# Weight conversion from the seventh head on, and two unread products per head instead of one

## The chip, the core and the metric

The program runs on one NeuronCore of a Trainium2 chip; the other seven are not used. The metric is device time in microseconds (us) of one execution, as the median of several runs. In the profile the engines are PE (TensorE, matrix products), DVE (VectorE), ACT (ScalarE), POOL (GpSimd) and SP (SyncE, which here only issues transfers). Each engine works off its own instructions in order; they wait for one another by semaphores.

## What is computed

Three layers: windowed causal attention with a linear bias, a dense layer with squared ReLU, and a layer with eight experts of which each token takes one.

```python
# attention: B, H, S, D = 4, 8, 576, 64; window of 128 positions
scores = scale * np.matmul(q, k.transpose(0, 1, 3, 2))
scores = np.where(mask, scores + bias[None], -1000000000.0)
scores = scores - np.max(scores, axis=-1, keepdims=True)
attn = np.exp(scores)
attn = attn / (np.sum(attn, axis=-1, keepdims=True) + 1e-09)
attn_out = np.matmul(attn, v)
...
# x: 2304 tokens x 512; w_in 512 x 2048, w_out 2048 x 512
h = x @ w_in
r = np.maximum(h, 0.0)
x = (s * (r * r) + b) @ w_out
...
# experts: each token goes to the expert of its largest logit, 512 -> 1024 -> 512
h = np.maximum(x[mask] @ w1[e], 0.0)
out[mask] = gate_w[mask, None] * (h @ w2[e])
```

## The kernel before

The 2304 tokens are 18 tiles of 128. Attention goes by units, one head of one tile: 144 units, eight per tile. One call of `tick` starts a unit and carries earlier ones on by a step each; the tick of unit n does:

- the score product of unit n (`stage_A`, L242, into one of the banks 0 to 3; two products where a unit looks at two key tiles),
- the value product of unit n-4 (`stage_D`, L301), the transposition of unit n-2 (`stage_C`, L278), and for every fourth unit a transposition of finished rows (`stage_T`, L330),
- on DVE the bias and minimum of the scores (`stage_B`, L254), on ACT the exponential with its sum (`stage_N`, L262) and the copy of the transposed weights (`stage_C2`, L283).

The dense weights come as 32 chunks of 512 KB (w_in and w_out by turns) and are held as a high and a low part. `conv_ops` gives four steps for a chunk: the load, issued by SP (L178), into one of four `stage` buffers; a cast on ACT (`cast`, L181); a shift on DVE (`d`, L185); the high part on ACT (L193) with the low part on DVE (L194), both in `e`. The queue `conv` holds these steps in order. `pt`, called seven times per tick in the first four tiles, adds `rate` to a counter and takes the next step from the queue whenever the counter passes one. The loads of the first four chunks are issued at the start, among those of the first tiles of q, k and v.

`warm(n)` issues n products of zeros, 128x512, into bank 3 (L747); nobody reads them, which is why they are called unread products here. Nine stand ahead of the first tick.

The first four ticks (`LEAD`) stand under `manual_schedule`, which keeps their instructions in the order of the text. Everything else of this stage may be moved by the scheduler: it puts an instruction on its engine where its own model of the time finds it ready, also ahead of instructions that the text has earlier. The ticks up to `ticks(2)`, 21 of them, go with nothing beside them; from then on the first dense products (`L1`, L351: twelve products for a block of w_in; `L2`, L374: six for a block of w_out) are mixed with two ticks per block. `need(c)` takes conversion steps until chunk c is done, before a product that reads it.

Of the kernel before, what the change touches and what calls it, by code (L numbers as in the profile page):

```python
# [43 lines left out]
def moe_attention_kernel(ctx, tc, qT, kT, vN, w_in, w_out, sc_s, sc_b, bneg, tri, bmix,  # L44
# [190 lines left out]
    def stage_A(u, S):  # L235
        t, h, order, sl, bc, n = geom(u)
        pr, odd = divmod(h, 2)
        hb = slice(64, 128) if odd else slice(0, 64)
        o = S[:, 0:n]
        if t < NRAW:  # L240
            for i, k in enumerate(order):
                nc.tensor.matmul(S[:, i * P:(i + 1) * P], lhsT=raws[1][t][hb, pr, :], rhs=raws[0][k][hb, pr, :], start=True, stop=True)  # L242
            return
        Q, K, L = (sp.QO, sp.KO, sp.LO) if odd else (sp.QE, sp.KE, sp.LE)
        nc.tensor.matmul(o, lhsT=Q[:, pr, :], rhs=K[:, pr, sl, :], start=True, stop=False)
        nc.tensor.matmul(o, lhsT=Q[:, pr, :], rhs=L[:, pr, sl, :], start=False, stop=True)

    def stage_B(u, S):
        t, h, order, sl, bc, n = geom(u)
        s, st = sbuf(u)[:, 0:n], st_r[u % 4]  # L250
        bi, c = (bias8[h], -0.125) if t < NRAW else (bias, 2.0 ** -(h + 1))
        if t in MIXED or t in AFTER_MIXED:
            bi, bc = bmx[t in AFTER_MIXED], slice(0, 256)
        nc.vector.tensor_tensor_reduce(s, S[:, 0:n], bi[:, bc], scale=c, scalar=3.0e38,  # L254
                                       op0=ALU.add, op1=ALU.min, accum_out=st[:, 0:1])
# [18 lines left out]
    def stage_C(u, PO):  # L274
        t, h, order, sl, bc, n = geom(u)
        p = sbuf(u) if t < NRAW else sp.p[u % 2]
        for i in range(len(order) if t < NRAW else 1):
            nc.tensor.transpose(PO[:, i * 128:(i + 1) * 128], p[:, i * 128:(i + 1) * 128], ident)  # L278
# [15 lines left out]
    def stage_D(u, PO):  # L294
        t, h, order, sl, bc, n = geom(u)
        last = len(order) - 1
        if t < NRAW:
            o = outs(u)[:, h % 4 * 64:(h % 4 + 1) * 64]
            for i, k in enumerate(order):
                v = raws[2][k].rearrange("p c f -> p (c f)")[:, h * 64:(h + 1) * 64]  # L300
                nc.tensor.matmul(o, lhsT=PW[u % 2][:, i * P:(i + 1) * P], rhs=v, start=i == 0, stop=i == last)  # L301
            return
        for i, k in enumerate(order):
            nc.tensor.matmul(PO[:, 0:P], lhsT=sp.V[k % 3][:, h // 2, :], rhs=PP[u % 2][:, t - k], start=i == 0, stop=i == last)

    def stage_X(u, PO, part=2):
        t, h = divmod(u, H)
        if t < NRAW:
            if h % 4 == 3 and part != 0:
                g = u // 4 % 2  # L310
                rs, xs = rs_r[g], xs_r[g]
                nc.vector.tensor_scalar(rs, su_r[t % 2][:, h - 3:h + 1], 1e-9, None, op0=ALU.add)
                nc.vector.reciprocal(rs, rs)
                nc.vector.tensor_tensor(xs.rearrange("p (h d) -> p h d", h=4), outs(u).rearrange("p (h d) -> p h d", h=4),
                                        rs.unsqueeze(2).to_broadcast([P, 4, 64]), op=ALU.mult)
            return
        pr, odd = divmod(h, 2)
        hb = slice(64, 128) if odd else slice(0, 64)
        blk, c = divmod(t, 2)
        xh, xl = (x[hb, pr, c * P:(c + 1) * P] for x in xbuf(blk))  # L320
        o = PO[hb, 0:P]
        if part != 1:
            nc.scalar.activation(xh, o, AF.Copy)
        if part != 0:
            nc.vector.tensor_tensor(xl, o, f32(xh), op=ALU.subtract)

    def stage_T(u):
        g = u // 4 % 2
        for i in range(2):
            nc.tensor.transpose(bank[4 + g][:, 256 + i * P:256 + (i + 1) * P], xs_r[g][:, i * P:(i + 1) * P], ident)  # L330

    def stage_Y(u):
        t, g = u // H, u // 4 % 2
        blk, c = divmod(t, 2)
        o = bank[4 + g][:, 256:512].rearrange("p (c t) -> p c t", c=2)
        xh, xl = (x[:, 2 * g:2 * g + 2, c * P:(c + 1) * P] for x in xbuf(blk))
        nc.scalar.activation(xh, o, AF.Copy)
        nc.vector.tensor_tensor(xl, o, f32(xh), op=ALU.subtract)
# [69 lines left out]
    def run(ops):  # L408
        for f in ops:
            if callable(f):  # L410
                f()
# [173 lines left out]
    rate, due = [0.0], [0.0]  # L585
# [9 lines left out]
    def plan_preps(t, h):  # L595

        if t < NRAW:
            return
        if h in (0, 1):
            preps.ops += prep_q(t, 2 + h)  # L600
            if h == 1 and t + 1 < NT:
                preps.ops.append(lambda: load_qkv(t + 1, 1))
        if t + 1 < NT:
            if h == HK:
                preps.ops += prep_k(t + 1)
                if t + 2 < NT:
                    preps.ops.append(lambda: load_qkv(t + 2, 0))
            if h == HV:
                preps.ops.append(lambda: load_qkv(t + 1, 2))
            if h in (5, 6):  # L610
                preps.ops += prep_q(t + 1, h - 5)
# [11 lines left out]
    def unit(n):  # L623

        n -= LAG if n >= NRAW * H + LAG else 0
        return n if 0 <= n < UN else None

    def ticks(t):

        return t * H + LAG + (LAG - 1 if t > NRAW else 0)  # L630

    OR0, OR, OR1 = 'BX.C.M.G.N...', '.BUC..VME.G[..R]', 'BUC.VE...MG[].R.'
    def tick(Sb, POb, mid=None, attend=True, Ob=None):
        n = nu[0] if attend else 2 * UN
        if attend:
            nu[0] += 1
        u, c, d, x = (None if NRAW * H <= i < NRAW * H + LAG else unit(i) for i in (n, n - 2, n - LAG + 1, n - LAG))
        if u is not None:
            S = Sb[u % len(Sb)]
            plan_preps(*divmod(u, H))  # L640
            stage_A(u, S)
        if d is not None:
            POd = Ob[d % len(Ob)] if Ob else POb[d % len(POb)][:, 256:512]
            stage_D(d, POd)
        if c is not None:
            POc = POb[c % len(POb)]
            stage_C(c, POc)
        turn = x is not None and x % 4 == 3 and x < NRAW * H
        if turn:
            stage_T(x)  # L650
        def B():
            if u is not None:
                stage_B(u, S)

        def X():
            if d is not None:
                stage_X(d, POd)

        def U():
            if d is not None:  # L660
                stage_X(d, POd, 0)

        def V():
            if d is not None:
                stage_X(d, POd, 1)

        def C():
            if c is not None:
                stage_C2(c, POc)

        def N():
            if u is not None:
                stage_N(u)
            if turn:
                stage_Y(x)

        def E():
            if u is not None:
                stage_N(u, 0)
            if turn:  # L680
                stage_Y(x)

        def R():
            if u is not None:
                stage_N(u, 1)

        def M():
            if mid is not None:
                mid(0)

        def G():
            if mid is not None:
                mid(fill if '[' in od else ())
            elif '[' in od:
                run(fill)

        fs = dict(E=E, R=R, U=U, V=V, B=B, X=X, C=C, N=N, M=M, G=G)
        od = OR0 if n < NRAW * H else (OR if mid is not None else OR1)
        fill = [pt if z == '.' else fs[z] for z in od[od.find('[') + 1:od.find(']')]] if '[' in od else []
        od = od[:od.find('[') + 1] + od[od.find(']') + 1:]  # L700
        for z in od:
            if z == '[':
                continue
            if z == '.':
                pt()
            else:
                fs[z]()
# [18 lines left out]
    HK, HV = 2, 5  # L726
    SK = 8
    J3 = 4
    LEAD = 4

    def need(c):
# [12 lines left out]
    def warm(n):  # L744

        for _ in range(n):
            nc.tensor.matmul(bank[3], lhsT=zero[:, 0:P], rhs=zero, start=True, stop=True)  # L747

    warm(9)
    with tc.manual_schedule():  # L750
        for i in range(LEAD):
            tick(*wide)
            warm(1)
            if i == 1:
                rate[0] = 0.17
    for i in range(LEAD, ticks(2)):
        tick(*wide)
        warm(1)
    rate[0] = 0.4
    for j in range(SK):  # L760
        def mid(i):
# [14 lines left out]
    for j in range(SK):  # L776
        first(1, j)
        if j >= J3:
            tick(**third_b)
# [6 lines left out]
        pt()  # L786
        if j == J3 - 1:
            while preps.ops:
# [312 lines left out]
```

## Time and profile before

| | |
|---|---|
| time of 3 runs, median (lowest to highest) | 914.15 us (914.04 to 915.16) |
| time of the profiled execution | 915.15 us |
| span in the profile, first to last instruction | 913.4 us |
| mean granted clock of PE over the span | 0.959 |
| PE busy | 896.0 us, 98% |
| ACT, DVE, POOL busy | 647.0, 642.2, 325.4 us |

The profile gives for a stretch of time the busy time of each engine and the granted clock of PE, as a share of full speed. Two levels occur: 1.00 is 2.4 GHz, 0.50 is 1.2 GHz; a number between them is a stretch with both. A row of the timeline is an instruction, or several alike run together (x4), with its start and its time; where the engine was idle ahead of it, the row ends with that idle time and what released the instruction. The time of a product in the timeline includes its way through the array, so consecutive products overlap; what a product costs in a row of products is the distance of two starts.

### The profile page before, as it was taken

The page shows a single profiled execution, that of the slowest core. Times are in us where ns is not written, and L with a number is a line of the kernel's source. Part 1 is how long each engine was busy: PE and PEld are TensorE (multiplying, and loading weights), DVE is VectorE, ACT ScalarE, POOL GpSimd, SP SyncE. Part 2 cuts the span into 40 slices and gives each one's busy share as a digit, 9 for nine tenths or more (in the row PEclk, how much of TensorE's full clock was granted, in tenths as well). Part 3 has the DMA queues.
Part 4 walks back from the last instruction along what each step waited for, and adds up shares of the span by engine and source line. Part 5 has one row for each costly group of instructions (what it writes and reads, how often), then busy time and mean ns, then how long its engine had stood idle before and what let it go on. Part 6 is the DMA issues. An engine that isn't in the chain of part 4 may idle for free. (4 is left out here: it accounts for less than half of the span.)

```text
span 913.4 us, 17128 instructions
## 1 busy us (share of the span) xinstructions
PE 896.0 (98%) x5341; PEld 777.2 (85%) x5344; DVE 642.2 (70%) x1719; ACT 647.0 (71%) x1501; POOL 325.4 (36%) x553
## 2 busy tenths in 40 slices
PE   7999998999999999999999999999999999999997
PEld 4678877989999999999999999988888888888886
DVE  3336789656665676667666655467989999899895
ACT  4447897656676767666776753457889889888885
POOL 2000246554663266555655642111632111111101
PEclk7558999999999999999999999999999999999999
DMA  7224652010020102011200200456973795755300
GB/s 263 74 70 134 227 161 78 13 59 13 25 59 13 59 24 59 21 31 44 58 16 33 36 1 1 168 184 227 268 262 127 267 338 212 257 187 210 110 20 29
DMA packets 31600, 101.32 MB, mean 111 GB/s; under 512 B 8581, under 2 KB 9222, under 8 KB 24850
## 3 DMA queue, kind: packets, MB, share of 16 engines
q1 hardware_dynamic: 26562, 89.58, 29.4%
q0 software_dynamic: 4256, 9.46, 2.9%
q10 hardware_dynamic: 688, 1.15, 0.3%
q8 instruction: 43, 0.70, 0.3%
q14 instruction: 51, 0.42, 0.2%
HBM read 133.82 MB, written 10.92 MB: 158 GB/s over the span
## 5 line engine op out<-in xcount | busy, mean ns | idle before, releaser
L351 PE MATMUL bank<-XH,WIH 128*128 128x256 f32 x576 | 173.3, 301 | 0.8 <-ACT r L361 0.8
L351 PE MATMUL bank<-XH,WIL 128*128 128x256 f32 x576 | 163.7, 284 | 0.0
L351 PE MATMUL bank<-XL,WIH 128*128 128x256 f32 x576 | 163.4, 284 | 0.0
L363 DVE SCALAR_TENSOR_TENSOR bank<-bank,s_sb,r 128x256 f32<-128x256 f32 x112 | 55.1, 492 | 108.6 <-ACT r L361 108.2
L374 PE MATMUL bank<-WOH,GH 128*128 128x512 f32 x288 | 118.9, 413 | 0.5 <-ACT GH L364 0.5
L374 PE MATMUL bank<-WOH,GL 128*128 128x512 f32 x288 | 115.5, 402 | 1.1 <-DVE GL L366 1.1
L374 PE MATMUL bank<-WOL,GH 128*128 128x512 f32 x288 | 114.7, 398 | 0.0
L351 PEld LDWEIGHTS bank<-XH,WIH 128*128 128x128 f32 x576 | 110.6, 192 | 3.0 <-ACT r L361 1.0
L351 PEld LDWEIGHTS bank<-XL,WIH 128*128 128x128 f32 x576 | 110.4, 192 | 1.9 <-issue 0.2
L351 PEld LDWEIGHTS bank<-XH,WIL 128*128 128x128 f32 x576 | 109.9, 191 | 0.0
L364 ACT ACTIVATE GH<-bank,b_sb 128x256 fp32r<-128x256 f32 x112 | 53.2, 475 | 69.5 <-DVE bank L363 69.5
L262 ACT ACTIVATE s<-s,st 128x256 f32<-128x256 f32 (+1 forms) x144 | 71.2, 494 | 20.9 <-DVE st L254 17.7
L361 ACT ACTIVATE r<-bank 128x256 f32<-128x256 f32 x144 | 54.0, 375 | 44.5 <-PE bank L351 42.5
L830 PE MATMUL bank<-WIH,XH 128*128 128x512 f32 x192 | 77.7, 405 | 0.0
L254 DVE CUSTOM_DVE_ANT_0 s<-bank,bias 128x256 f32<-128x256 f32 (+1 forms) x112 | 44.7, 400 | 46.3 <-PE bank L242 32.5
L832 PE MATMUL bank<-WIL,XH 128*128 128x512 f32 x192 | 75.8, 395 | 0.0
L831 PE MATMUL bank<-WIH,XL 128*128 128x512 f32 x192 | 75.7, 394 | 0.0
L975 POOL DMA_INDIRECT out<-x,ids x23 | 28.1, 1223 | 133.4 <-ACT XH L959 109.3
L272 POOL TENSOR_SCALAR p<-p,st 128x128 f32<-128x128 f32 x104 | 42.5, 408 | 85.7 <-DVE st L265 69.7
L830 PE MATMUL bank<-WOH,XH 128*128 128x512 f32 x176 | 71.2, 405 | 0.0
L832 PE MATMUL bank<-WOL,XH 128*128 128x512 f32 x176 | 69.5, 395 | 0.0
L831 PE MATMUL bank<-WOH,XL 128*128 128x512 f32 x176 | 69.4, 394 | 0.0
(190 smaller groups left out, 2361.6 us busy)
## 6 DMA issues: line engine op xcount, KB each, us to landing
W1R<-w SPq DMA_DIRECT2D x46, 1024.0 KB
W2R<-w SPq DMA_DIRECT2D x46, 1024.0 KB
stage<-w_in SPq DMA_DIRECT2D x16, 512.0 KB
stage<-w_out SPq DMA_DIRECT2D x16, 512.0 KB
raw<-kT SPq DMA_DIRECT2D x18, 256.0 KB
raw<-qT SPq DMA_DIRECT2D x18, 256.0 KB
x1d<-stage SPq DMA_DIRECT2D x7, 512.0 KB
V<-vN SPq DMA_DIRECT2D x10, 256.0 KB
```

The source lines that it names most:

```text
L254: nc.vector.tensor_tensor_reduce(s, S[:, 0:n], bi[:, bc], scale=c, scalar=3.0e38, op0=ALU.add, op1=ALU.min, accum_out=st[:, 0:1])
L262: nc.scalar.activation(s, s, AF.Exp, bias=st[:, 0:1], scale=-1.0, accum_out=su)
L272: nc.gpsimd.tensor_scalar(p, p if n > P else s, st[:, 3:4], 1.0, op0=ALU.mult, op1=ALU.mult)
L351: nc.tensor.matmul(o, lhsT=w[j][:, c * P:(c + 1) * P], rhs=x[:, c, :], start=n == 0, stop=n == 11)
L361: nc.scalar.activation(r, o, AF.Relu)
L363: nc.vector.scalar_tensor_tensor(q, x, s_sb, r, op0=ALU.mult, op1=ALU.mult)
L364: nc.scalar.activation(gh, q, AF.Identity, bias=b_sb)
L374: nc.tensor.matmul(acc[k], lhsT=a[:, ts], rhs=w[j], start=(j == 0 and i == 0), stop=(j == NF - 1 and i == 2))
L830: nc.tensor.matmul(o, lhsT=lh, rhs=hi, start=first, stop=False)
L831: nc.tensor.matmul(o, lhsT=ll, rhs=hi, start=False, stop=False)
L832: nc.tensor.matmul(o, lhsT=lh, rhs=lo, start=False, stop=last)
L975: nc.gpsimd.indirect_dma_start(out=out[:, :], out_offset=bass.IndirectOffsetOnAxis(ids[:, 0:1], 0), in_=y, in_offset=None, bounds_check=NT ...
```

## The change

Conversion no longer begins in the third tick but in the seventh (`CONV = 6`, counted from zero), at a rate of 0.25 steps per call of `pt` instead of 0.17; the rate in the ticks behind this stage is as it was. Each of the first 21 ticks is followed by two unread products instead of one. In the new text all conversion of this stage is asked for outside the four ticks of `manual_schedule`. Line numbers behind L729 grow by one: the unread products are L747 before and L748 after.

```diff
@@ -726,6 +726,7 @@
     HK, HV = 2, 5
     SK = 8
     J3 = 4
+    CONV = 6
     LEAD = 4
 
     def need(c):
@@ -750,12 +751,12 @@
     with tc.manual_schedule():
         for i in range(LEAD):
             tick(*wide)
-            warm(1)
-            if i == 1:
-                rate[0] = 0.17
+            warm(2)
     for i in range(LEAD, ticks(2)):
+        if i == CONV:
+            rate[0] = 0.25
         tick(*wide)
-        warm(1)
+        warm(2)
     rate[0] = 0.4
```

What the scheduler makes of it shows in the order of the instructions on each engine. ACT at the start of the program, before; `stage_95` and `stage_96` are the buffers of the first chunk of w_in and the first of w_out, `s_...` the scores of a unit, `PW_...` copies of transposed weights:

```order
L535 ACTIVATE su_184<-half 128x2
L262 ACTIVATE s_165,su_184<-s_165,st_167 128x128
L262 ACTIVATE s_166,su_184<-s_166,st_168 128x128
L181 ACTIVATE tmp_156<-stage_96 128x512
L283 ACTIVATE PW_190<-bank_82 128x128
L262 ACTIVATE s_192,su_184<-s_192,st_169 128x128
L181 ACTIVATE tmp_155<-stage_95 128x512
```

The same place of ACT after:

```order
L535 ACTIVATE su_184<-half 128x2
L181 ACTIVATE tmp_155<-stage_95 128x512
L193 ACTIVATE WIH_113<-stage_95 128x512
L262 ACTIVATE s_165,su_184<-s_165,st_167 128x128
L262 ACTIVATE s_166,su_184<-s_166,st_168 128x128
L283 ACTIVATE PW_190<-bank_82 128x128
L262 ACTIVATE s_192,su_184<-s_192,st_169 128x128
L181 ACTIVATE tmp_156<-stage_96 128x512
```

Before, two exponentials come first and then the cast of the second chunk; after, the cast and the high part of the first chunk come ahead of the first exponential, and the cast of the second chunk follows the third one.

DVE at the start of the program after (before, the two upper conversion rows stand further down, behind the fifth and the sixth score reduction):

```order
L530 MEMSET zero 128x256
L185 SCALAR_TENSOR_TENSOR stage_95<-stage_95,tmp_155 128x512
L194 TENSOR_TENSOR WIL_121<-stage_95,WIH_113 128x512
L254 ISA s_165,st_167<-bank_78,bias_176 128x128
L254 ISA st_167 128x1
```

The shift and the low part of the first chunk now stand ahead of the first score reduction.

PE around its second value product (`PW_191`), before; `bank_81` takes the unread products, `zero` is their operand:

```order
L242 MATMUL bank_79<-raw_0_194,raw_0_197 128x128
L301 MATMUL bank_85<-raw_0_200,PW_191 128x64
L278 MATMUL bank_85<-ident,s_165 128x128
L747 LDWEIGHTS zero
L747 MATMUL bank_81<-zero 128x512
L242 MATMUL bank_80<-raw_0_194,raw_0_197 128x128
L278 MATMUL bank_82<-ident,s_166 128x128
L301 MATMUL bank_85<-raw_0_200,PW_190 128x64
L747 LDWEIGHTS zero
L747 MATMUL bank_81<-zero 128x512
```

PE at the same value product after, from the last two of four unread products in a row:

```order
L748 LDWEIGHTS zero
L748 MATMUL bank_81<-zero 128x512
L748 LDWEIGHTS zero
L748 MATMUL bank_81<-zero 128x512
L301 MATMUL bank_85<-raw_0_200,PW_191 128x64
L278 MATMUL bank_85<-ident,s_165 128x128
L748 LDWEIGHTS zero
L748 MATMUL bank_81<-zero 128x512
L748 LDWEIGHTS zero
L748 MATMUL bank_81<-zero 128x512
L278 MATMUL bank_82<-ident,s_166 128x128
L301 MATMUL bank_85<-raw_0_200,PW_190 128x64
```

The two score products between these steps have moved ahead of them, and the unread products have come closer together: four, two and (behind the last row) two more, with two short steps between each.

## Rows read from the trace of the kernel before

**Rows 1.** The page: PE's busy total, and granted clock in 40 slices (tenths).

```profile
PE 896.0 (98%) x5341; PEld 777.2 (85%) x5344; DVE 642.2 (70%) x1719; ACT 647.0 (71%) x1501; POOL 325.4 (36%) x553
...
PEclk7558999999999999999999999999999999999999
```

**Rows 2.** Stretches: length, busy us (count) of PE PEld DVE ACT POOL; clock, DMA.

```profile
8.70:12.30 3.60, 0.02 (x1) 0.00 (x0) 0.09 (x1) 0.90 (x3) 0.00 (x0) 1.00 1.04 417
...
14.00:30.00 16.00, 15.64 (x50) 9.99 (x50) 5.88 (x24) 7.54 (x26) 0.00 (x0) 0.50 0.48 163
30.00:62.80 32.80, 32.09 (x118) 24.15 (x121) 11.16 (x38) 14.31 (x41) 0.00 (x0) 0.50 0.22 67
62.80:72.30 9.50, 9.50 (x39) 8.16 (x40) 4.58 (x11) 5.48 (x13) 0.00 (x0) 0.50 0.25 72
...
77.40:100.00 22.60, 22.53 (x152) 18.88 (x152) 18.39 (x48) 19.39 (x48) 0.00 (x0) 1.00 0.57 180
```

**Rows 3.** Timeline of PE: start, us, instruction, and idle time before it.

```profile
8.39 0.33 PE L278 MATMUL bank<-ident,s 128*128 128x128 f32 x1
12.35 0.56 PE L301 MATMUL bank<-raw,PW 128*128 128x64 f32 x2 [3.63 <-ACT PW L283]
...
16.80 0.47 PE L278 MATMUL bank<-ident,s 128*128 128x128 f32 x1
```

**Rows 4.** Timeline of ACT: two steps of conversion.

```profile
11.40 0.77 ACT L181 ACTIVATE tmp<-stage 128x512 f16<-128x512 bf16 x1 [3.81 <-DMA stage<-w_out]
...
14.28 0.66 ACT L193 ACTIVATE WIH<-stage 128x512 fp32r<-128x512 f32 x1
```

**Rows 5.** Stretches around a later idle time of PE.

```profile
150.00:151.90 1.90, 0.00 (x0) 0.02 (x1) 1.87 (x5) 1.85 (x6) 1.82 (x4) 1.00 0.03 9
...
152.50:155.80 3.30, 3.30 (x11) 2.72 (x10) 2.10 (x6) 2.53 (x7) 3.07 (x7) 0.50 0.14 47
155.90:158.00 2.10, 2.10 (x19) 2.06 (x19) 1.97 (x10) 0.48 (x2) 0.96 (x3) 1.00 0.45 163
```

**Rows 6.** Timeline of PE: first and last of six dense products; another first.

```profile
73.81 0.63 PE L374 MATMUL bank<-WOH,GH 128*128 128x512 f32 x1
...
75.94 0.63 PE L374 MATMUL bank<-WOH,GL 128*128 128x512 f32 x1
...
152.46 0.78 PE L374 MATMUL bank<-WOH,GH 128*128 128x512 f32 x1
```

**Rows 7.** Timeline of SP: an issue.

```profile
8.02 0.33 SPq L546 DMA_DIRECT2D b_sb<-sc_b  x1
```

**Rows 8.** SP's waits up to 30 us: what that issue waited for.

```profile
SPq L546 <- DMA stage<-w_in: 1.2, 1, 1.2
```

**Rows 9.** Timeline of DVE: first score reduction; two steps of conversion.

```profile
6.03 0.29 DVE L254 CUSTOM_DVE_ANT_0 s<-bank,bias 128x128 f32<-128x128 f32 x1 [4.90 <-POOL bias L553]
...
12.21 0.69 DVE L185 SCALAR_TENSOR_TENSOR stage<-stage,tmp 128x512 uint32<-128x512 uint32 x1 [4.41 <-ACT tmp L181]
...
15.26 0.69 DVE L194 TENSOR_TENSOR WIL<-stage,WIH 128x512 fp32r<-128x512 f32 x1
```

**Rows 10.** Timeline of PE: one head at half clock, score product to unread product.

```profile
47.54 1.22 PE L242 MATMUL bank<-raw,raw 64*128 64x128 f32 x4
...
50.02 0.63 PE L747 MATMUL bank<-zero 128*128 128x512 bf16 x1
```

**Rows 11.** Timeline of PE: the steps of a head at full clock.

```profile
82.86 0.71 PE L242 MATMUL bank<-raw,raw 64*128 64x128 f32 x4
...
84.13 0.37 PE L351 MATMUL bank<-XH,WIH 128*128 128x256 f32 x1
```

**Rows 12.** Timeline of PE: first product of three blocks of w_in.

```profile
62.81 0.56 PE L351 MATMUL bank<-XH,WIH 128*128 128x256 f32 x1
...
72.38 0.56 PE L351 MATMUL bank<-XH,WIH 128*128 128x256 f32 x1
...
90.11 0.37 PE L351 MATMUL bank<-XH,WIH 128*128 128x256 f32 x1
```

## The prediction

> **What bounds the kernel now.** First the page: PE is busy for 98% of the span, so what PE has to do sets the time, unless its clock is low. The line of the granted clock has its only long low stretch at the start [rows 1]. The stretches show it: from 14.00 to 62.80 and on to 72.30 the clock is 0.50, its lower level (1.2 GHz), while PE is busy nearly throughout and ACT less than half of the time; from 77.40 it is 1.00 (2.4 GHz) [rows 2]. So for some 65 us the kernel is bound by PE at half clock. That is the stage the change touches: the first 21 heads (16 of the first two tiles and 5 behind them) and the first dense products after them.
>
> How the clock was lost is in the timeline. PE stops behind a transposition of 8.39 and starts again at 12.35, after 3.63 us of waiting for ACT [rows 3]. In 8.70 to 12.30 it is idle, still at 1.00, and afterwards the clock is 0.50 [rows 2]. ACT in that time stood before the cast of a conversion (L181), waiting until 11.40 for a weight load [rows 4]; the copy L283 that PE's row names was queued behind it. A shorter hole far later confirms the pattern: PE idle in 150.00 to 151.90, then 152.50 to 155.80 at 0.50, then 1.00 again [rows 5]. What ran before a return: six 512-column products back to back, 73.81 to 75.94, start to start 2.13/5 = 0.426 us [rows 6]; the clock is 1.00 from about 77.4. The same products begin at 152.46 [rows 6] and lead to the return by 155.90 [rows 5]. Heads with one unread product each, and later heads mixed with L351, ran from 14.00 to 72.30 without a return [rows 2].
>
> One rule of the Trainium skill would tell this otherwise. "TensorE: Matmul & The Clock Gate", Part 1, says that "the default state is throttled, and activity releases the throttle". Here a busy PE (15.64 of 16.00 us and 32.09 of 32.80 [rows 2]) was not released. By the rule alone half clock would end soon after each restart, which is the second rival below; by the rows it matters what PE is busy with.
>
> **The change, part by part.**
>
> (1) The start of conversion. The text puts it at the seventh head, but the order of the changed kernel has the first conversion whole (cast, shift, high part, low part) at the head of ACT and DVE, ahead of the first softmax. So the blocked ACT does not go away. The first weight load has landed when SP's waiting issue starts at 8.02; the wait's releaser is that load [rows 7, 8]. Then, in series, cast 0.77 and high part 0.66 on ACT [rows 4], shift 0.69 and low part 0.69 on DVE [rows 9]: 8.1 to 8.9, 9.6, 10.3, 11.0. Only then comes the first score reduction (L254, 6.03 now [rows 9]), 0.29 long, and PE's fourth score product needs its bank. PE restarts at about 11.4 instead of 12.35. It stopped not later than now (8.39 + 0.33), about 7.6 by its shorter list (three score products, four unread ones): a hole of 2.7 us at least, 3.8 by count. The hole at 150.00 was 1.90, so the clock falls again. I count no gain from the moved start but the restart, 0.95 us.
>
> (2) Lateness. Ahead of the hole the old order also ran two score products and two transpositions that now come after it. Six such products of a wide head take 50.02 - 47.54 = 2.48 us at half clock, 0.41 each [rows 10], so 1.65 us. Between restart and the transposition of the fifth head there are eight unread products instead of three: 5 x 0.426 = 2.13. That transposition, at 16.80 now [rows 3], comes at 16.80 - 0.95 + 1.65 + 2.13 = 19.6.
>
> (3) What the doubled products do to the clock. Between restart and 19.6 the new order has four unread products in a row, a value product, a transposition, two unread, a transposition, a value product, two unread: eight of 0.426, 3.4 us, in about 4.6 us. Nothing between 14.00 and 73.81 is like it in the trace (one unread product stands there after 2.48 us of head steps [rows 10], and the L351 are broken up by head steps). It is nearer to the dense products that stood ahead of the two returns than to the 58 us that brought none. I take the return to 1.00 to fall in or right behind this cluster, at 19.6; bounds: at the restart (11.4) and not before the dense products (72 to 87). This is the main choice of the forecast; the trace does not show this mix.
>
> (4) The rest of the stage at full clock. From 16.80 to the first L351 at 62.81 [rows 3, 12] PE needs 46.0 us now, 15 unread products within it (6.4 us), 39.6 without. The head steps shrink from 2.48 to 84.13 - 82.86 = 1.27 [rows 10, 11], factor 0.51: 20.3 us. The 30 unread products that remain cost half of 0.426 each, 6.4: 26.7 us. The second product per head, so, costs 3.2 us here. ACT, off the path now, is nearly late next: busy 7.54 + 14.31 us in 14.00 to 62.80 [rows 2], plus the greater rate of conversion (15 heads x 7 x 0.25 = 26.3 steps instead of 19 x 7 x 0.17 = 22.6; 3.7 steps at about 0.7, from 0.77 and 0.66 [rows 4]): about 24 us. In 77.40 to 100.00 ACT was busy 19.39 of 22.60 and PE still never idle [rows 2]; at that share 24 us need 28. I take 28 (26.7 if ACT hides, 30 if PE waits a little for each copy). First L351 at 19.6 + 28 = 47.6 instead of 62.81: 15.2 us gained.
>
> (5) The first dense stage. From L351's start of one weight block to the next at half clock: 72.38 - 62.81 = 9.57; at full clock 90.11 - 84.13 = 5.98 [rows 11, 12]. The 14.6 us from 62.81 to 77.4 shrink by the factor 0.625: 5.5 us gained. No cost for weights: their loads go ahead as before on SP's queue and DMA is not full there.
>
> (6) Conversion is about one weight block further when the heads end; this relieves ACT later by at most 0.77 + 0.66 = 1.4 us, in a stage that PE bounds at 22.53 of 22.60. I take 0 and keep 1.4 for the lower end.
>
> Sum: 915.15 (profiled execution, span 913.4 and 1.75 around it) - 15.2 - 5.5 = 894.5. The profiled execution lies 1.0 above the median shown, within the spread of the runs. I round to 895.
>
> **Rivals.**
>
> A, slower: no return in the heads. Then all the unread products after the hole, 38 instead of 18, run at half clock on a PE that is the bound: 20 x 0.426 = 8.5; plus 1.65, less 0.95: the first L351 at 72.0, 9.2 us late. The clock comes back with dense products. In the new order the twelve L351 of the first block are unbroken, so it may come 4 to 12 us earlier in the sequence than now, worth 0.375 of that, 1.5 to 4.5. Time 919.5 to 924, middle 922. It decides whether the clock is 1.00 or 0.50 between 20 and 60 us. For it: 58 us of busy PE without a return. Against it: no dense cluster stood in them.
>
> B, faster still: full clock soon after the restart, as the skill's sentence quoted above has it, or no fall in the hole. The 8.2 us from 11.4 to 19.6 then shrink by about 0.4: 891. Against it: rows 2 and 5.
>
> C: the clock returns in the cluster, PE runs ahead of ACT, waits for a copy or for a load that ACT waits for (as in rows 4), and falls to half again for a part of the heads. Half of the gain of (4) lost: 902 to 910. Against it: from 77.40 to 100.00 the kernel kept 1.00 with ACT at 86% [rows 2].
>
> D, the change does what it says: no conversion ahead of the first softmax, no hole at all. The order excludes it.
>
> **How the numbers follow.** Forecast with return in the cluster 0.58 (889 to 902: return some 4 us earlier or later at 0.4, ACT's bounds, the 1.4 of (6)); A 0.24; B 0.08; C 0.08; D 0.02. The cases of both signs hold much, so the range reaches from B's lower end, 888, to the middle of A, 922; what is left out is the upper half of A and a little below. Faster by over 0.2% (about what a measurement of this kernel can tell from no change): all but A and a little of C, 0.73. Within 0.2%: 0.03. Slower: 0.24.
>
> **What would show it.** In the profile after: ACT's first L181 at about 8.1 and the first L254 at about 11.0; PE idle until 11.4; clock 0.50 behind that; 1.00 again by 16 to 23; the first L351 near 48; the stages behind 100 us unchanged but some 20 us earlier. If the clock stays at 0.50 until L351, step 3 is wrong and A holds, and each unread product shows 0.43 start to start. If PE never idles early, step 1 is wrong. If 1.00 holds but the first L351 is later than 52, ACT's share in step 4 is wrong.

## The result and the profile after

| | before | after |
|---|---|---|
| median (lowest to highest) | 914.10 us (913.08 to 915.16) | 890.95 us (890.56 to 891.63) |
| profiled execution | 915.15 us | 890.56 us |
| span; mean granted clock | 913.4 us; 0.959 | 888.8 us; 0.992 |

The ratio is 0.9747 [0.9731, 0.9764]: 23 us faster, 4 us below the forecast of 895 and inside its range. In all the times below a ratio leaves out the executions that lie over 1.5% above the fastest of their kernel; the medians and ranges count them.

PE's busy total has become smaller although the change adds 21 products, and the low slices of the clock at the start are nearly gone. The page after (compare [rows 1]):

```profile
PE 874.3 (98%) x5365; PEld 759.5 (85%) x5365; DVE 641.5 (72%) x1719; ACT 647.3 (73%) x1501; POOL 321.4 (36%) x553
...
PEclk8999999999999999999999999999999999999999
```

Stretches after, with the columns of [rows 2]:

```profile
8.00:10.00 2.00, 0.00 (x0) 0.00 (x0) 1.28 (x2) 0.66 (x1) 0.22 (x1) 1.00 1.04 421
...
11.00:12.00 1.00, 1.00 (x5) 0.26 (x3) 0.00 (x0) 0.90 (x5) 0.00 (x0) 0.71 1.03 352
12.00:14.00 2.00, 2.00 (x8) 1.49 (x8) 0.66 (x5) 1.47 (x7) 0.00 (x0) 0.50 0.16 35
...
18.00:20.00 2.00, 2.00 (x12) 1.29 (x12) 1.27 (x4) 1.47 (x6) 0.00 (x0) 0.94 1.04 374
...
30.00:40.00 10.00, 10.00 (x66) 6.92 (x64) 7.48 (x21) 8.62 (x23) 0.00 (x0) 1.00 0.30 84
...
127.50:130.80 3.30, 3.30 (x12) 2.73 (x11) 3.17 (x9) 2.84 (x8) 3.06 (x5) 0.50 0.01 2
```

The hole is there (no PE work in 8.00 to 10.00). The clock falls behind it: 0.71 in 11.00 to 12.00 is full clock until 11.00 + (0.71 - 0.50)/0.50 = 11.42, then 0.50. It is back soon: 0.94 in 18.00 to 20.00 is half clock for 2 x (1 - 0.94)/0.50 = 0.24 us, so the return lies at 18.24. From there on it is 1.00 up to 127.5, where a stretch at 0.50 follows an idle time of PE, as at 152.5 before [rows 5]; another of the same length stands at 574.7 to 578.0 (before at 599.6 to 603.0). Half clock behind the hole lasted 6.8 us instead of the 65 us of [rows 2].

PE after (restart, the cluster, one head at full clock, and the first dense product), then ACT, SP and DVE during the hole:

```profile
10.44 0.70 PE L242 MATMUL bank<-raw,raw 64*128 64x128 f32 x4 [3.14 <-DVE st L254]
...
14.46 1.89 PE L748 MATMUL bank<-zero 128*128 128x512 bf16 x4
...
16.67 1.06 PE L748 MATMUL bank<-zero 128*128 128x512 bf16 x2
17.52 0.42 PE L278 MATMUL bank<-ident,s 128*128 128x128 f32 x1
...
18.06 0.70 PE L748 MATMUL bank<-zero 128*128 128x512 bf16 x2
...
28.57 0.71 PE L242 MATMUL bank<-raw,raw 64*128 64x128 f32 x4
...
29.93 0.59 PE L748 MATMUL bank<-zero 128*128 128x512 bf16 x2
30.45 0.71 PE L242 MATMUL bank<-raw,raw 64*128 64x128 f32 x4
...
45.51 0.36 PE L351 MATMUL bank<-XH,WIH 128*128 128x256 f32 x1
```

```profile
6.95 0.78 ACT L181 ACTIVATE tmp<-stage 128x512 f16<-128x512 bf16 x1 [4.27 <-DMA stage<-w_in]
8.79 0.66 ACT L193 ACTIVATE WIH<-stage 128x512 fp32r<-128x512 f32 x1 [1.06 <-DVE stage L185]
```

```profile
6.88 0.33 SPq L546 DMA_DIRECT2D b_sb<-sc_b  x1
```

```profile
SPq L546 <- DMA stage<-w_in: 0.7, 1, 0.7
```

```profile
7.77 0.99 DVE L185 SCALAR_TENSOR_TENSOR stage<-stage,tmp 128x512 uint32<-128x512 uint32 x1 [6.63 <-ACT tmp L181]
9.48 0.69 DVE L194 TENSOR_TENSOR WIL<-stage,WIH 128x512 fp32r<-128x512 f32 x1 [0.72 <-ACT WIH L193]
10.09 0.28 DVE L254 CUSTOM_DVE_ANT_0 s<-bank,bias 128x128 f32<-128x128 f32 x1
```

In the cluster the pair of 16.67 takes 1.06 us, a half-clock distance of 0.43; the pair of 18.06, the last of the cluster, takes 0.70. The conversion of the first chunk stands ahead of the first score reduction, in series between ACT and DVE from 6.95 to 10.1, and PE waits for it.

### The profile page after: what moved, and what is told of

It is laid out like the page before. It is cut to its first block, busy times and chain, and to the rows that moved or that the text cites. A ratio compares the mean times of both kernels' runs of the same rounds, so it can differ in the third digit from the quotient of the medians.

```text
span 888.8 us, 17171 instructions
## 1 busy us (share of the span) xinstructions
PE 874.3 (98%) x5365; PEld 759.5 (85%) x5365; DVE 641.5 (72%) x1719; ACT 647.3 (73%) x1501; POOL 321.4 (36%) x553
## 5 line engine op out<-in xcount | busy, mean ns | idle before, releaser
L351 PE MATMUL bank<-XH,WIH 128*128 128x256 f32 x576 | 172.3, 299 | 1.0 <-ACT r L361 0.8
L351 PE MATMUL bank<-XH,WIL 128*128 128x256 f32 x576 | 163.0, 283 | 0.0
L351 PE MATMUL bank<-XL,WIH 128*128 128x256 f32 x576 | 162.2, 282 | 0.0
L351 PEld LDWEIGHTS bank<-XH,WIH 128*128 128x128 f32 x576 | 109.3, 190 | 4.0 <-ACT r L361 2.2
L351 PEld LDWEIGHTS bank<-XL,WIH 128*128 128x128 f32 x576 | 109.6, 190 | 1.5
L351 PEld LDWEIGHTS bank<-XH,WIL 128*128 128x128 f32 x576 | 108.9, 189 | 0.2
L374 PEld LDWEIGHTS bank<-WOH,GL 128*128 128x128 f32 x288 | 54.5, 189 | 15.2 <-DVE GL L366 3.4
```

The source lines that it names most:

```text
L351: nc.tensor.matmul(o, lhsT=w[j][:, c * P:(c + 1) * P], rhs=x[:, c, :], start=n == 0, stop=n == 11)
L374: nc.tensor.matmul(acc[k], lhsT=a[:, ts], rhs=w[j], start=(j == 0 and i == 0), stop=(j == NF - 1 and i == 2))
```

## The experiments

All of them compute the same outputs; lines are those of the changed kernel, or of the kernel before where a version is made from that. The question was fourfold: which of the two parts of the change brings the gain, what about the unread products brings the clock back, whether they are needed afterwards, and what the hole costs. The kernel before, run again beside them, had medians from 912.2 to 914.1 us; a difference of 1 or 2 us between versions that ran at different times says little.

**The conversion part alone.**

```diff
-            warm(2)
+            warm(1)
...
-        warm(2)
+        warm(1)
```

> The changed kernel with one unread product per head instead of two: the conversion part of the change alone. Theory (clock lost in the early hole, brought back by the dense cluster of unread products): ACT and DVE start with the first conversion as in the changed kernel, PE idles until about 10.4 us, the clock is 0.50 from there to the first dense blocks, first L351 at 60 to 63 us, time 911 to 915 us. Rival (the moved conversion makes the gain, by a freer ACT): clock back within the heads, 890 to 896 us.

Measured 906.64 us (904.55 to 913.57, seven runs), ratio 0.994 [0.9906, 0.9974]. The profiled execution (910.38) has the hole (PE waits 3.9 us for L254), and stretches like those of before:

```profile
20.00:40.00 20.00, 20.00 (x73) 14.29 (x72) 7.57 (x26) 8.16 (x27) 0.00 (x0) 0.50 0.27 85
...
70.00:80.00 10.00, 10.00 (x59) 8.38 (x59) 8.14 (x19) 7.15 (x17) 0.00 (x0) 0.88 0.48 166
```

Half clock stays until about 72. The moved conversion alone is worth 0.6%, and it doesn't remove the hole. The stretches are those that were expected; the median is 4.4 us below the expected 911 to 915.

**The doubled products alone** (the kernel before with both of its `warm(1)` made `warm(2)`).

```diff
-            warm(1)
+            warm(2)
...
-        warm(1)
+        warm(2)
```

> The kernel before with two unread products per head: the other part alone, conversion from the third head at 0.17. In its order three exponentials and a copy come ahead of the first cast on ACT, so the wait for the first chunk (landed by 7 to 8 us) blocks little. Theory: the hole shrinks to under 1.5 us or goes, the clock stays at 1.00 or returns in the cluster of four, two and three unread products; 885 to 892 us. Rival (the moved conversion makes the gain): half clock to the dense blocks and 20 unread products more on it, 919 to 924 us.

Measured 883.64 us (883.23 to 883.88), ratio 0.9681 [0.9647, 0.9714]: better than the whole change by 7.3 us. There is no hole. The only wait of PE up to 60 us is the one at the opening:

```profile
PE bank L747 <- DVE zero L530: 1.2, 1, 1.2
```

The timeline of ACT in this kernel shows where the first cast stands:

```profile
8.64 0.28 ACT L283 ACTIVATE PW<-bank 128x128 f32<-128x128 f32 x1 [0.50 <-PE bank L278]
...
9.20 0.77 ACT L181 ACTIVATE tmp<-stage 128x512 f16<-128x512 bf16 x1
```

The cast stands behind the first copy and the third exponential, and finds its load landed: it has no idle time ahead of it. Before, a cast stood ahead of that copy and waited until 11.40 [rows 4]; that was the cast of the second chunk, whose load is issued later, while here the first cast is that of the first chunk, as the expectation above read it from the order (the row doesn't name the chunk). With more work on PE the scheduler gave the cast a later place. So in the whole change the two parts work against each other: the conversion part puts a blocking step first, and the doubled products are paid for bringing the clock back. Of the 7.3 us between the two kernels 5.1 are there at the first dense product (L351 at 40.40 here, 45.51 in the whole change, with the same head steps ahead of it). The waiting of 3.14 and half of the 6.8 us at half clock, 3.4, would make 6.5; the opening, where the distance of the products falls to 0.21 at about 6.5 us here and at 4.6 in the whole change, takes about 1 off the difference. The other 2.2 come later; the stretches at 0.50 of 127.5 and 574.7 are missing in this profile, which reads 1.00 from 60 to 880.

**Two products in the first nine heads, then one** (of the changed kernel).

```diff
-        warm(2)
+        warm(2 if i < 9 else 1)
```

> The changed kernel, two unread products behind the first nine heads, one behind the other twelve. Theory (once back, the clock is kept by what the heads do with one product): 1.00 from about 18 us on, twelve products of 0.21 less on PE, 888 to 891 us. Rival (two per head are needed to keep it): falls to 0.50 again between 20 and 45 us, 896 to 908 us.

Measured 887.62 us (884.98 to 889.18), ratio 0.9714 [0.9676, 0.9751]; 3.3 us less than the whole change. The hole is there (3.4), the return at about 19.7, and behind it the clock is kept with one product per head:

```profile
16.00:20.00 4.00, 4.00 (x14) 2.18 (x12) 1.48 (x6) 1.52 (x6) 0.00 (x0) 0.54 0.95 335
20.00:40.00 20.00, 20.00 (x131) 14.70 (x130) 12.94 (x44) 16.17 (x50) 0.00 (x0) 1.00 0.37 113
```

**Two in the first nine heads, then none.**

```diff
-        warm(2)
+        warm(2 if i < 9 else 0)
```

> The changed kernel with two unread products in the first nine heads and none in the twelve behind them (these products are read by nothing). Theory: the clock returns in the cluster of eight unread products as in the version with two and then one (by about 20 us), and PE that runs its heads back to back does not need unread products to keep it; then a further 12 x 0.213 = 2.6 us fall away where PE bounds, so 885 us, or 887 to 888 where ACT's copies come next to bound the heads. Rival: without unread products PE runs ahead of ACT and DVE, stands still for a copy, and the clock falls again: 0.50 for a part of the heads and 895 to 910 us.

Measured 885.25 us (883.13 to 895.98, four runs), ratio 0.9728 [0.9665, 0.9791]. With a longer hole in the profiled execution (4.5 us) the return comes at 21.1; then PE is never idle for long and the clock stays without any unread product:

```profile
20.00:22.00 2.00, 2.00 (x8) 1.07 (x7) 0.70 (x4) 1.20 (x5) 0.00 (x0) 0.72 0.73 278
...
30.00:40.00 10.00, 10.00 (x71) 8.21 (x69) 5.96 (x24) 7.36 (x23) 0.00 (x0) 1.00 0.20 63
```

The median is 2.4 us below the version with two and then one, near to the 12 x 0.213 = 2.6 of twelve products fewer, but the executions of the two versions overlap. The rival, a second fall, isn't in this profile. The execution of 895.98 wasn't profiled; its mean granted clock is 0.979, that of the profiled one 0.992, so it spent about 2 x (0.021 x 894 - 0.008 x 885) = 23 us more at half clock. Half of that is about the 12 us that it took longer than the two at 883. Whether its clock came back late or fell a second time isn't shown.

**One product in the first nine heads, then two.**

```diff
-            warm(2)
+            warm(1)
...
-        warm(2)
+        warm(1 if i < 9 else 2)
```

> The changed kernel with one unread product behind each of the first nine heads and two behind the other twelve: no dense cluster behind the hole, but two per head later. Theory (the cluster brings the clock back): 0.50 until the dense blocks, the first L351 at 64 to 68 us (twelve products of 0.43 more than with one throughout), 908 to 916 us. Rival (two per head in any place bring it back): 1.00 from 25 to 40 us on, 893 to 903 us.

Measured 909.23 us (897.11 to 914.35, eight runs), ratio 0.987 [0.9837, 0.9903]. The profiled execution (913.89) stays at half clock through nearly all of the heads:

```profile
30.00:60.00 30.00, 30.00 (x107) 21.07 (x107) 10.34 (x33) 13.16 (x36) 0.00 (x0) 0.50 0.23 74
...
66.00:67.00 1.00, 1.00 (x6) 0.88 (x6) 0.00 (x0) 0.46 (x1) 0.00 (x0) 0.67 0.95 377
```

```profile
67.41 0.36 PE L351 MATMUL bank<-XH,WIH 128*128 128x256 f32 x1
```

The return lies at 66.00 + (1 - 0.67)/0.50 = 66.66, among the last heads and ahead of the first dense product: two products per head did bring the clock back here, without a cluster, after some 40 us of such heads. Four of the eight executions lie between 897 and 905, four at 914, of which the profiled one is one. The mean granted clock of 897.11 and 899.29 is 0.981 and 0.980, that of the profiled one 0.963: about 35 us at half clock in place of 67. These two are 15 to 17 us shorter than the profiled one, about half of the difference, so half clock was shorter in them, as the rival has it; where it ended isn't shown. For 904.40 and 904.56 the mean is 0.997, but it is 0.998 for the three others at 914, so it decides nothing there. Together with the two versions ahead this says: where the order makes a cluster the return came at 18 to 21 us in all three profiles; with two products per head and no cluster it came too, but late in the profile, and half clock didn't last equally long in each execution.

**Unread products of half the width** (behind the heads 128x256 instead of 128x512; the opening ones are unchanged).

```diff
-            nc.tensor.matmul(bank[3], lhsT=zero[:, 0:P], rhs=zero, start=True, stop=True)
+            c = 512 if nu[0] == 0 else 256
+            nc.tensor.matmul(bank[3][:, 0:c], lhsT=zero[:, 0:P], rhs=zero[:, 0:c], start=True, stop=True)
```

> The changed kernel, but each unread product behind a head is 128x256 instead of 128x512: two per head as in the change, with the columns of one. Hole and order at the start as in the changed kernel. Theory (what brings the clock back is how densely the cluster fills PE with such columns, and this cluster is half as long): no return in the heads, 0.50 to the dense blocks, first L351 at 60 to 64 us, 904 to 914 us. Rival (it is the number of unread products, or their place): back by 18 to 22 us, 884 to 892 us.

Measured 913.20 us (911.73 to 914.90, eight runs), ratio 1.0006 [0.9986, 1.0026]: the gain is gone.

```profile
12.00:70.00 58.00, 58.00 (x230) 44.72 (x229) 22.52 (x75) 27.86 (x84) 0.00 (x0) 0.50 0.33 101
...
75.00:77.00 2.00, 2.00 (x8) 1.12 (x6) 0.00 (x0) 0.48 (x2) 0.00 (x0) 0.51 0.44 176
```

The return moves from 18.24 to 77. As many unread products are issued, but not at the same places: with shorter products the scheduler put score products between them again, and the cluster is gone. PE from the four products in a row on (in the changed kernel no L242 stands between 14.46 and 18.68):

```profile
14.03 1.06 PE L749 MATMUL bank<-zero 128*128 128x256 bf16 x4
15.02 0.79 PE L242 MATMUL bank<-raw,raw 64*128 64x128 f32 x2
...
16.43 0.64 PE L749 MATMUL bank<-zero 128*128 128x256 bf16 x2
17.00 0.79 PE L242 MATMUL bank<-raw,raw 64*128 64x128 f32 x2
```

So the number of unread products as such doesn't bring the clock back; whether their width or their place does can't be told from this version, because both changed. Half-width products in the order of the change were not run. By the rule of the Trainium skill ("TensorE: Matmul & The Clock Gate", Part 1) that activity releases the throttle, a PE busy for 58.00 of 58.00 us should have been released; this trace speaks against the sentence in that short form.

**Nine heads in the order of the text.** With `LEAD = 9` and the new rate set inside that loop, the first conversion can't be put ahead of the first heads.

```diff
-    LEAD = 4
+    LEAD = 9
...
         for i in range(LEAD):
+            if i == CONV:
+                rate[0] = 0.25
             tick(*wide)
```

> The changed kernel with the order of the text kept for nine heads instead of four, so that the first conversion stands behind the first softmaxes on ACT and DVE, as the text of the change says. Theory (the hole costs its idle 3.1 us and, by the low clock behind it, about half of the 6.6 us from 11.4 to 18.0): no idle time of PE above 1.5 us, 1.00 from the opening on, first L351 at 39 to 42 us, 884 to 888 us. Rival (the hole is paid back, since ACT is late with its conversion and bounds the heads): first L351 at 44 to 46 us, 889 to 892 us.

Measured 886.08 us (885.85, 886.31, 884.83 and one of 921.9), ratio 0.9701 [0.9656, 0.9745]. In the profiled execution (885.85) there is no hole, the longest wait of PE between the opening and 60 us is 0.27 us, and the clock column is 1.00 up to 567; the pairs of unread products behind the heads take 0.59 to 0.60 us from 5.29 on, which is full clock.

**The same with one product per head.**

```diff
-            warm(2)
+            warm(1)
...
-        warm(2)
+        warm(1)
```

> The order of the text for nine heads, as in the run with that edit, but one unread product per head: no hole at the start, no cluster. Theory (the hole is what loses the clock, and one product per head is enough to keep it): 1.00 throughout, time 882 to 886 us. Rival (one product per head cannot keep the clock in the narrow first heads, with or without the hole): falls to 0.50 within 20 us, 905 to 915 us.

Measured 880.05 us (879.35, 877.43, 880.74 and one of 900.88), ratio 0.9633 [0.9584, 0.9682]. No half clock between 6 and 562 us, and the waits of PE in the first 60 us are these:

```profile
PE bank L748 <- DVE zero L530: 1.2, 1, 1.2
PE bank L748 <- DVE st L254: 0.3, 1, 0.3
```

The number of unread products is that of before; the order of the first ticks differs, and the start and the rate of the conversion. Without the hole one product per head keeps the clock. The second product costs 6.0 us between the medians of these two versions, against 21 x 0.213 = 4.5 of PE time; in the whole change a pair takes 30.45 - 29.93 = 0.52 us, which would make 5.5. The rest isn't traced.

**The doubled products alone, then one** (the kernel before with two products in nine heads and one behind them).

```diff
-            warm(1)
+            warm(2)
...
-        warm(1)
+        warm(2 if i < 9 else 1)
```

> The kernel before with two unread products behind the first nine heads and one behind the other twelve, conversion as before. Theory: no hole, 1.00 throughout, PE saves twelve products of 0.21 against two throughout (883.6): 881 to 883 us, if PE bounds the heads; 883 to 885 if ACT does. Rival (one per head does not keep the clock later on): falls between 20 and 40 us, 890 to 900 us.

Measured 884.07 us (883.14 to 888.59 and one of 909.67), ratio 0.9682 [0.9637, 0.9727]: no gain over the doubled products alone, though the same step had saved 3.3 us in the changed kernel. The profiled execution (888.59) shows another start:

```profile
5.87 1.04 PE L747 MATMUL bank<-zero 128*128 128x512 bf16 x2
...
13.32 1.89 PE L747 MATMUL bank<-zero 128*128 128x512 bf16 x4
...
15.54 1.49 PE L747 MATMUL bank<-zero 128*128 128x512 bf16 x3
...
18.97 0.61 PE L747 MATMUL bank<-zero 128*128 128x512 bf16 x2
```

Four products take 1.89 us, a distance of 0.43: half clock, from the opening until behind the cluster of four and three. The same pair in the kernel without "then one" took 0.90 at 5.86 and 0.60 at 7.11:

```profile
5.86 0.90 PE L747 MATMUL bank<-zero 128*128 128x512 bf16 x2
...
7.11 0.60 PE L747 MATMUL bank<-zero 128*128 128x512 bf16 x2
```

So whether the nine opening products bring the clock up before the heads differs between executions. The return behind this cluster is the fourth of its kind in the profiles, and the only one without a hole ahead of it. Why the executions at 883 gain nothing isn't settled. The execution of 909.67 has a mean granted clock of 0.963, some 67 us at half clock, as the kernel before has; so it lost the clock behind the opening, and what took it isn't shown.

**A longer opening** (`LEAD = 9`, one product per head, 14 opening products).

```diff
-    warm(9)
+    warm(14)
```

> The version with nine ticks in the order of the text, conversion from the seventh head at 0.25 and one unread product per head, with fourteen unread products ahead of the first tick instead of nine. Theory: what differs between the executions of that version (877.4 to 880.7, and one of 900.9) is whether the nine opening products bring the clock up before the heads begin; five more make the opening longer by 5 x 0.213 to 5 x 0.426 = 1.1 to 2.1 us, but the first scores wait for the bias anyway (their bank is read from about 6 us on), so 878 to 881 us in every execution. Rival: the opening is not what differs, a hole of another origin is; then an execution of 895 or more comes again among them.

Measured 879.64 us (878.56 to 881.47, five runs), ratio 0.9637 [0.9614, 0.966]: the same median, as foretold, and no execution near 900. After the opening the pair of score products runs at full clock:

```profile
7.12 0.48 PE L242 MATMUL bank<-raw,raw 64*128 64x128 f32 x2
```

Five runs without a long one, where it had been one in four, agree with the theory of the opening but don't prove it; the execution of 909.67 above shows that a long one can have another origin. This and the version with nine opening products are the fastest, 11 us below the change.

## Why the prediction was right, step by step

The sum was made for the profiled execution: 894.5 forecast, 890.56 measured. The 3.9 us between them: 2.1 in steps (1) and (2), 0 in step (4), 0.5 in step (5), 1.3 behind it.

**Step (1), the hole stays: right, its end forecast 1.0 too late.** PE restarts at 10.44, forecast 11.4. The cast began at 6.95, not at 8.1, because the load landed earlier in this execution: SP's issue that waits for it (L546) starts at 6.88, at 8.02 before [rows 7]. The landing isn't the same in all executions, and the forecast took it over from one. In the five other versions with the first conversion at the head it comes between 7.34 and 8.43, and PE restarts 3.25 us behind it in each (7.34 and 10.59, 7.69 and 10.94, 8.00 and 11.25, 8.27 and 11.52, 8.43 and 11.68); so the chain of the forecast is what PE waits for. Here it is 3.56: the shift took 0.99 us instead of 0.69, and why isn't shown. From the cast to the first score reduction it is 10.09 - 6.95 = 3.14 us, forecast 2.9. The hole, by chance of the same length, 3.14, lies in the forecast 2.7 to 3.8, and the clock fell.

**Step (2), lateness: 7.1 us from restart to the fifth head's transposition, forecast 8.2.** The list of instructions was right; the clock was still full until 11.42, so 1.0 us of the stretch did the work of 2.0. The transposition came at 17.52 instead of 19.6.

**Step (3), the return in the cluster: right, and the main choice.** The clock came back at 18.24, at the last pair of the cluster. In the versions with two, then one, and two, then none, the same order brought it back at 19.7 and 21.1. The conversion part alone, the version with half the width and the profile of one, then two, lack the cluster; there it came back at 72, 77 and 66.7. That it needs the cluster is more than these runs show: the half-width version changed the order together with the width, and one, then two, had its return in the heads, and two executions of it spent some 30 us less at half clock than the profile.

**Step (4), the rest of the heads: 45.51 - 17.52 = 28.0 us, forecast 28, by luck.** The forecast added 1.3 us to PE's own 26.7 because ACT, at its share, would hold PE up. It didn't: PE is busy 10.00 of 10.00 us in 30.00 to 40.00 with ACT at 8.62, and it never waits between 17.52 and 45.51. PE's own work took the 28. At full clock a head of 28.57 to 30.45 is 1.36 us of steps and 0.52 for two unread products, forecast 1.27 and 0.43; and the clock was still half up to 18.24. So the term for the second product (3.2) was somewhat small: 0.26 each, not 0.213. Taking it away from twelve heads gained 3.3 between the medians and 1.4 between the profiled executions, and nothing in the kernel before with its products doubled.

**Step (5), the first dense stage: 6.0, forecast 5.5.** The rows of the activation behind L351, third block, before and after:

```profile
82.08 0.40 ACT L361 ACTIVATE r<-bank 128x256 f32<-128x256 f32 x1
```

```profile
58.74 0.39 ACT L361 ACTIVATE r<-bank 128x256 f32<-128x256 f32 x1
```

23.3 us earlier, of which 17.3 were there at the first L351 (62.81 [rows 12] against 45.51).

**Step (6), nothing behind it: mis-sized by 1.3.** Seven blocks on, the same row stands 25.1 us earlier, at the end of the execution 24.6. Before and after:

```profile
117.58 0.38 ACT L361 ACTIVATE r<-bank 128x256 f32<-128x256 f32 x1
```

```profile
92.53 0.36 ACT L361 ACTIVATE r<-bank 128x256 f32<-128x256 f32 x1
```

The idle time of PE that stands at 151.91 before has its like here, shorter by 0.7 and with another releaser. Before and after:

```profile
151.91 0.46 PE L304 MATMUL bank<-PP,raw 128*128 128x128 f32 x2 [1.92 <-POOL PP L289]
```

```profile
126.83 0.46 PE L304 MATMUL bank<-PP,raw 128*128 128x128 f32 x2 [1.22 <-DVE sm L392]
```

But the 1.7 us between the third block and the tenth were gained ahead of it, and behind it the lead is 25.1 as well (157.16 against 132.10), so the shorter idle time is not where they come from. Between the third and the tenth block ACT has less of the conversion to do. The high parts alone (L193; ACT's busy us and count, clock, DMA), before and after:

```profile
82.08:117.58 35.50, 8.07 (x13) 1.00 0.70 224
```

```profile
58.74:92.53 33.79, 6.70 (x10) 1.00 0.68 225
```

That is 1.4 us less, as much as step (6) named and put at nothing. That PE gained its 1.7 us by this is likely and not shown.

**The rivals.** A did not happen, but two versions without the cluster do what it says: half clock to the dense products in the conversion part alone and with half the width. Its price wasn't met in a profile: with half the width the unread work is about that of before, and so is the time, 913.2; the one execution of 921.9 of the version with nine heads in the order of the text and two wide products per head lies at A's price, but was not profiled. B gave 891, which is the time measured, and is still not what happened: 12.00 to 18.00 ran at 0.50. B's number came out of 2.1 us in (1) and (2), of which 1.1 are a load that landed earlier in this execution, 0.5 in (5) and 1.3 in (6), all with the same sign; only the profile tells B from the forecast. C (a second fall in the heads) didn't come: the clock is 1.00 from 30.00 to 40.00 with ACT at 86%. D was excluded rightly by the new order, but the prediction doesn't ask what either part would do alone. There the larger finding lay: the doubled products alone have no hole.

## What to carry to other kernels

When a clock is lost in one hole at the start, look first at what stands ahead of the engine that PE waits for, and take the hole away: keeping the order of the first heads brought 880 us with as many unread products as before. When work is added to buy a clock back, look at where it lands in the order: here eight wide unread products close together were followed by the return at 18 to 21 us, while two per head, mixed with the steps of the heads, were followed by it at 66.7 us in one profile. A change of two parts is worth taking apart; here one part alone was 7 us better than both, because the scheduler answered the other part by putting the blocking step first. And an experiment that changes the length of an instruction may change the order too: compare the order before reading the result.

## What the runs showed of the chip that I had not expected

- The clock at the opening isn't the same in all executions. Nine products of 512 columns, 0.43 us apart at first, were followed by full clock at once in one profile (a pair of 0.60 us at 7.11) and by half clock until 17 in another. In the other profiles of this case full clock came between 4 and 7 us. Single executions of 900.88, 909.67 and 921.9 appeared in versions whose profiles have no hole, against 877 to 889 for the others; that the opening makes them long is not shown, and for 909.67 the mean granted clock (0.963) speaks against it. The Trainium skill ("TensorE: Matmul & The Clock Gate", Part 1) says that the first rise varies from run to run by about 0.5 us; here the profiles differ by some 11 us (from 6.5 to 17).
- The recorded clock can't be trusted ahead of its first change, nor can its mean where such a change is missing (0.997 for that profile). In the profile with half clock until 17 the column says 1.00 for the same time; the distance of the products (0.43 against 0.21) decides:

```profile
12.00:16.00 4.00, 4.00 (x15) 2.30 (x15) 2.37 (x11) 2.04 (x9) 0.00 (x0) 1.00 0.55 134
```

- The fall doesn't come at the same place in a hole: in the changed kernel PE was idle from 7.3 to 10.44, and the clock was full until 11.42, 1.0 us into the work that followed; in the conversion part alone PE was idle from 6.7 to 10.59, and the clock fell at 7.6, 1 us into the hole.
